# Scores of three batches as float16 products of stacked halves, with operands transposed by DMA

## The chip, the core and the metric
The kernel runs on one NeuronCore of a Trainium2 chip. The core has five engines, each with a queue of its own that it works off in order: TensorE (PE, matmuls, results in PSUM), VectorE (DVE), ScalarE (ACT), GpSimd (POOL, which cannot reach PSUM) and SyncE (SP), which here issues every DMA. The metric is the device time of one execution in microseconds (us).

## What is computed
Causal attention for 4 batches of 12 heads, then an MLP with a squared ReLU:

```
batch, n_heads, seq, head_dim = (4, 12, 448, 64)
scores = scale * np.matmul(q, k.transpose(0, 1, 3, 2))      # causal mask: -1e9 above the diagonal
attn = np.exp(scores - max);  attn = attn / (sum + 1e-09)
x = np.matmul(attn, v)  ->  (batch * seq, n_heads * head_dim) = (1792, 768)
h = x @ w_in;  r = np.maximum(h, 0.0);  g = r * r           # w_in is 768 x 2048
out = g @ w_out                                             # w_out is 2048 x 768, all float32
```

## The kernel before
**Pairs.** Attention goes by pairs of heads: 6 per batch, 24 in all, numbered i. A sequence of 448 is cut into 4 blocks of 112 rows. For a pair, `pair_load` fetches q, k and v into the tile `raw` (two sets, used in turn); `pair` transposes q and k on PE (L570, four blocks each) into PSUM and copies them out as float32 (`qT`, `kT`, L538 on ACT or L539 on DVE). In these tiles head 0 of the pair lies on partitions 0 to 63 and head 1 on 64 to 127.

**Scores and softmax.** For block c the scores of both heads, (c+1)*112 columns wide, are two float32 matmuls over 64 partitions each (L594), one in either half of the array's rows. The trace shows each as two entries. DVE adds the mask and takes the row's extreme in one custom instruction (L599), ACT takes the exponential and its sum (L603). The result is scaled and split into a float16 high half (`hi`) and a low half (`lo`) in the tile `psrc`; a DMA transposition (L556) turns both halves of a head into `pT`. The values (L651) are three float16 products: high by high, high by low, low by high. Batch 0 does without DMA transpositions and halves: it transposes float32 on PE (L629) and multiplies in float32 (L641).

**MLP.** Tokens go in sub-blocks of 256 or 128 columns, eight in all. The first layer (L918) is 16 units of 18 float16 matmuls; each unit is followed by ReLU (L929), square (L936 or L938) and the split into halves `g` (`hi` L397 on ACT, `lo` L405). The second layer (L954) is matmuls of 384 columns. Weights are loaded as raw words, narrowed (L721 to L736) and split, before the first sub-block can start.

**Who sets the order.** Every piece is handed to a planner (`Plan`) with its cost on each engine that may do it, what it reads and writes, and a due time. `Plan.order` lists the pieces by a model of the queues; the due times and a bias per engine come from the table `PR`. A split may go to ACT, DVE or POOL (`hi`), or DVE or POOL (`lo`); the planner picks. On POOL a low half of a scaled source is two instructions (L413 and L415). For SP the planner reckons a time `ISSUE` that an issue holds the queue, longer for the transpositions of pT. What it has ordered stands fixed in the program.

Of the kernel before, what the change touches and what calls it, by code (L numbers as in the profile page):

```python
# [29 lines left out]
    "m_L2": 2404805, "m_fac": -4350124, "m_ghi": 179886, "m_glo": -223927, "m_msq": 1943718, "m_ob": 5617141,  # L30
    "m_relu": -2665863, "m_sig": 3771052, "m_sq": -634180, "m_tau": 1847951, "wi_wl": 351942, "wi_wn": -1179075,
    "wi_wq": 1731582, "wo_wl": 2402465, "wo_wn": -983095, "wo_wq": -76879, "ws_wn": 4319096, "wt_wn": 1234225,
    "a0_P.copy@act": -2272, "a0_P.copy@dve": 3583, "a0_P.nrm@act": -308, "a0_P.nrm@dve": 3448, "a0_P.nrm@pool": -1037,
    "a0_qk.copy@act": -4902, "a0_qk.copy@dve": -890, "a0_x.top@act": 4549, "a0_x.top@dve": 5350,
    "m_ghi.hi@act": -5477, "m_ghi.hi@dve": -2320, "m_ghi.hi@pool": -5555, "m_glo.lo@dve": -384,
    "m_glo.lo@pool": -5962, "m_relu.@act": -4403, "m_relu.@dve": 5641, "m_sq.@act": -2058, "m_sq.@dve": 782,
    "m_sq.@pool": -1987, "ws_wn.hi@act": -3852, "ws_wn.hi@dve": -6000, "ws_wn.hi@pool": -3283, "ws_wn.lo@dve": -212,
    "ws_wn.lo@pool": 3600, "wt_wn.hi@act": -2079, "wt_wn.hi@dve": -3096, "wt_wn.hi@pool": -1467,
# [27 lines left out]
class Plan:  # L66
# [3 lines left out]
    ISSUE = {False: 475.0, True: 650.0}  # L70

    def __init__(self):
        self.ops = []
        self.heavy = set()
        self.last_w = {}
        self.last_r = {}
        self.rings = {}
        self.spots = {}
        self.port = []
        self.bias = []  # L80
        self.kind = []
# [63 lines left out]
    def order(self):  # L145
# [31 lines left out]
        warm, busy, edge = False, 0.0, self.WINDOW  # L177
        while done < n:
# [38 lines left out]
            if e == "sp":  # L217
                free[e] = t + self.ISSUE[i in self.heavy]
# [64 lines left out]
def attention_relu2_kernel(  # L283
# [32 lines left out]
    GB = [7]  # L316

# [18 lines left out]
    n_kT = maker("kT", 2)  # L336
    n_p32 = maker("p32", 2)
    n_pT = maker("pT", 3)
# [7 lines left out]
    n_l3 = maker("l3", 2)  # L346
# [15 lines left out]
    n_s = lambda b, j: spot(f"s{j}{b == 0}", SB[b == 0][j])  # L362
# [14 lines left out]
    junk = const.tile([128, VN // NPAIR], BF16, name="junk")  # L377
# [6 lines left out]
    def one(e, ns, fn, reads, writes, due, heavy=False, port=False):  # L384
        i = plan.add({e: ns}, fn, reads, writes, due, port=port)
        if heavy:
            plan.heavy.add(i)
# [663 lines left out]
```

## Time and profile before
| | us |
|---|---|
| median of 3 runs | 713.72 (710.7 to 714.43) |
| profiled execution | 715.77 |
| its span, first to last instruction | 714.0 |
| mean granted TensorE clock, share of full speed | 0.943 |

The span is cut below into stages. Busy time is the union of what an engine's instructions took. PEld is PE's weight load, which runs beside its matmuls. The granted clock (PEclk) is a share of 2.4 GHz; it is 1.2 GHz where it is 0.5.

### The profile page before, as it was taken

The page shows a single profiled execution, that of the slowest core. Times are in us where ns is not written, and L with a number is a line of the kernel's source. Part 1 is how long each engine was busy: PE and PEld are TensorE (multiplying, and loading weights), DVE is VectorE, ACT ScalarE, POOL GpSimd, SP SyncE. Part 2 cuts the span into 40 slices and gives each one's busy share as a digit, 9 for nine tenths or more (in the row PEclk, how much of TensorE's full clock was granted, in tenths as well). Part 3 has the DMA queues.
Part 4 walks back from the last instruction along what each step waited for, and adds up shares of the span by engine and source line. Part 5 has one row for each costly group of instructions (what it writes and reads, how often), then busy time and mean ns, then how long its engine had stood idle before and what let it go on. Part 6 is the DMA issues. An engine that isn't in the chain of part 4 may idle for free.

```text
span 714.0 us, 13829 instructions
## 1 busy us (share of the span) xinstructions
PE 658.6 (92%) x5182; PEld 465.0 (65%) x5182; DVE 325.8 (46%) x933; ACT 423.7 (59%) x1211; POOL 266.9 (37%) x382
## 2 busy tenths in 40 slices
PE   5877776799999899999999999999989899999998
PEld 3554544587666666787757756767656778776864
DVE  4999799889884555316320235123633110200000
ACT  2788978789876774774546664348645524414410
POOL 4232333215410326468348654447545202202200
PEclk9876767689999999999999999999999899999999
DMA  9997767545476664443365345435451300000000
GB/s 249 290 279 283 262 236 264 133 91 110 86 134 135 135 125 99 96 85 81 80 127 115 66 97 108 85 59 98 96 96 47 61 2 12 12 12 23 12 12 33
DMA packets 184866, 79.04 MB, mean 111 GB/s; under 512 B 173792, under 2 KB 179680, under 8 KB 184800
## 3 DMA queue, kind: packets, MB, share of 16 engines
q1 hardware_dynamic: 184800, 78.17, 45.7%
q8 instruction: 40, 0.66, 0.4%
q14 instruction: 26, 0.21, 0.1%
HBM read 45.81 MB, written 5.51 MB: 72 GB/s over the span
## 4 chain that ended last, share of the span: by engine, by line
PE 66%; DVE 14%; DMA 9%; POOL 5%; issue 3%; ACT 2%; SPq 1%; POOLq 0%; ACTq 0%; DVEq 0%
PE bank L918 27%; PE bank L954 23%; DMA pT<-psrc 7%; PE bank L594 5%; PE bank L651 4%; DVE bank L599 3%; PE bank L570 2%; DVE wo L724 2%; POOL p L413 2%; POOL psrc L415 2%; PE bank L641 2%; DVE wi L724 1%; DMA xt<-in_moe_w_out_dram 1%; DVE psrc L410 1%; DVE wo L721 1%
## 5 line engine op out<-in xcount | busy, mean ns | idle before, releaser
L918 PE MATMUL bank<-xt,wi 128*128 128x256 f16 (+1 forms) x2304 | 235.5, 262 | 0.0
L954 PE MATMUL bank<-wo,g 128*128 128x384 f16 x1344 | 228.8, 326 | 0.0
L918 PEld LDWEIGHTS <-wi 128*128 128x128 f16 x2304 | 201.5, 99 | 36.6 <-issue 14.3
L954 PEld LDWEIGHTS <-g 128*128 128x128 f16 x1344 | 128.2, 98 | 89.9 <-issue 10.0
L405 POOL TENSOR_TENSOR g<-g,g 128x256 f16<-128x256 f32 (+1 forms) x128 | 82.0, 650 | 197.2 <-ACT g L397 101.7
L599 DVE CUSTOM_DVE_ANT_0 bank<-bank,mask 112x112 f32<-112x112 f32 (+1 forms) x192 | 82.3, 472 | 128.8 <-PE bank L594 126.7
L603 ACT ACTIVATE p<-bank,nm 112x112 f32<-112x112 f32 (+1 forms) x192 | 93.3, 491 | 65.8 <-DVE nm L599 38.4
L594 PE MATMUL bank<-kT,qT 64*112 64x112 f32 (+3 forms) x384 | 78.0, 464 | 7.4 <-ACT p L603 4.4
L929 ACT ACTIVATE r<-bank 128x256 f32<-128x256 f32 (+1 forms) x128 | 45.0, 354 | 58.9 <-PE bank L918 58.0
L964 ACT ACTIVATE ob<-bank,fac 128x384 f32<-128x384 f32 x28 | 16.2, 579 | 82.5 <-PE bank L954 82.4
L397 ACT ACTIVATE psrc<-p,nm 112x448 f16<-112x448 f32 (+3 forms) x140 | 63.6, 524 | 0.4 <-ACT p L603 0.2
L415 POOL TENSOR_TENSOR psrc<-p,psrc 112x112 f16<-112x112 f32 (+3 forms) x76 | 53.8, 707 | 6.3
L936 ACT ACTIVATE g<-r 128x256 f32<-128x256 f32 (+1 forms) x122 | 46.8, 388 | 11.7 <-POOL g L405 7.0
L413 POOL TENSOR_SCALAR p<-p,nm 112x112 f32<-112x112 f32 (+3 forms) x76 | 43.5, 572 | 26.8 <-ACT psrc L397 26.8
L397 ACT ACTIVATE g<-g 128x256 f16<-128x256 f32 (+1 forms) x123 | 46.0, 386 | 10.7 <-PE bank L954 8.9
L594 PEld LDWEIGHTS bank<-kT,qT 64*112 64x112 f32 x384 | 31.4, 180 | 27.8 <-ACT p L603 10.9
L651 PE MATMUL bank<-pT,vp 112*64 112x336 f16 (+3 forms) x432 | 34.7, 295 | 12.2 <-DMA pT<-psrc 12.2
L410 DVE SCALAR_TENSOR_TENSOR psrc<-p,nm,psrc 112x336 f16<-112x336 f32 (+3 forms) x68 | 37.7, 592 | 10.5 <-ACT psrc L397 7.0
L651 PEld LDWEIGHTS <-vp 112*64 112x64 f16 x432 | 24.6, 114 | 24.3 <-issue 19.6
L603 ACT ACTIVATION_READ_ACCUMULATOR p<-bank,nm 112x1 f32 x192 | 38.1, 198 | 0.0
L736 POOL TENSOR_TENSOR wo<-wo,l 128x512 int32<-128x512 int32 (+1 forms) x16 | 20.0, 1253 | 44.3 <-DVE wo L724 9.2
L629 PE MATMUL bank<-ident,p 112*112 112x112 f32 x120 | 28.2, 394 | 6.2 <-ACT p L530 4.3
(120 smaller groups left out, 641.3 us busy)
## 6 DMA issues: line engine op xcount, KB each, us to landing
raw<-in_moe_w_out_dram SPq DMA_DIRECT2D x8, 768.0 KB, 5.1
xt<-in_moe_w_out_dram SPq DMA_DIRECT2D x8, 768.0 KB, 5.4
xt<-in_moe_w_in_dram SPq DMA_DIRECT2D x11, 512.0 KB, 6.2
out_dram<-ob SPq DMA_DIRECT2D x28, 192.0 KB, 2.0
raw<-in_moe_w_in_dram SPq DMA_DIRECT2D x9, 512.0 KB, 6.6
vn<-in_v_dram SPq DMA_DIRECT2D x18, 224.0 KB, 3.9
raw<-in_q_dram SPq DMA_DIRECT2D x36, 112.0 KB, 2.4
raw<-in_k_dram SPq DMA_DIRECT2D x36, 112.0 KB, 2.7
```

The lines of the kernel that those rows point to most:

```text
L397: nc.scalar.activation(out=o, in_=i, func=ACTF.Copy, scale=s)
L405: return plan.add({"dve": dve_ns(n), "pool": pool2_ns(n)}, lambda e: engines[e].tensor_tensor(out=out(), in0=in_(), in1=top(), op=ALU.subt ...
L413: nc.gpsimd.tensor_scalar(out=in_(), in0=in_(), scalar1=scale(), scalar2=1.0, op0=ALU.mult, op1=ALU.mult)
L415: nc.gpsimd.tensor_tensor(out=out(), in0=in_(), in1=top(), op=ALU.subtract)
L594: nc.tensor.matmul(out=ss[j].ap[0:P, 0:w], lhsT=q32.ap[r, c * P:w], rhs=k32.ap[r, 0:w], start=True, stop=True)
L599: one("dve", dve_ns(w, 1, 1) - 10, lambda e, c=c, w=w, s=s, j=j: nc.vector.tensor_tensor_reduce(out=s.ap[0:P, 0:w], in0=s.ap[0:P, 0:w], in ...
L603: one("act", act_ns(w, True, 1, True), lambda e, c=c, w=w, b0=b0, s=s, j=j: nc.scalar.activation(out=p32[j].ap[:, b0:b0 + c + 1, :].rearra ...
L651: nc.tensor.matmul(out=pv.ap[j * D:(j + 1) * D, kc * P:S], lhsT=vp.ap[:, hv, vb:vb + D], rhs=pT[j].ap[0:P, hp * NSL + x:hp * NSL + x + w, ...
L918: nc.tensor.matmul(out=h.ap[:, 0:n], lhsT=wi_hl(ci, hw)[:, ms], rhs=x[:, kd, hx, off:off + n], start=(kd == 0 and hw == 0 and hx == 0), st ...
L929: nc.scalar.activation(out=r.ap[:, 0:n], in_=h.ap[:, 0:n], func=ACTF.Relu)
L936: nc.scalar.activation(out=g32.ap[:, 0:n], in_=r.ap[:, 0:n], func=ACTF.Square)
L954: nc.tensor.matmul(out=o.ap[:, 0:HALF], lhsT=g[:, kf, hg, tt * 128:(tt + 1) * 128], rhs=wo_hl(kf, hw)[:, hh * HALF:(hh + 1) * HALF], start ...
```

## The change
For batches 1 to 3 (`F16S`) the scores become float16 products. Batch 0 stays as it was.

- `pair_norm`: the sums of squares of q and k of a pair (two Squares on ACT), added over partitions by a float32 matmul of two columns, give two powers of two; the score scale becomes a value in a tile (`sc`) instead of a number in the instruction.
- q and k, scaled by these, are split into halves (`qs`: 64 columns high, 64 low per head and block). A DMA transposition each makes `qT` and `kT`, whose 128 partitions are the high half stacked on the low half of one head. Two more DMAs write a copy of `kT` with the halves swapped.
- Each score block of each head is then two float16 matmuls over all 128 partitions, one with `kT` and one with the swapped copy. Each has one PSUM bank of two that are used in turn, instead of one bank per head.
- q and k are loaded by one DMA each, not two. `pT` has 2 buffers instead of 3. The third place of the narrowing (`l3`) now lies in the tile `qs`.
- The planner reckons 3500 ns for the issue of a pT transposition (650 before), 1300 for one of q or k, 650 for a swap, and 93 ns (`TURN`) whenever PE goes to or from a split array.
- The table `PR` has new numbers throughout, so that the whole order and the choice of engines are new.

```diff
...
-    "bias_dve": 329, "bias_act": -2161, "bias_pool": -229, "T0": -215719, "RAMP": 92933, "B1": 32241, "S1": 125326,
+    "bias_dve": -299, "bias_act": -4977, "bias_pool": 5919, "T0": -127481, "RAMP": 67524, "B1": 235234, "S1": 65078,
...
-    ISSUE = {False: 475.0, True: 650.0}
+    ISSUE = 475.0
+    TURN = 93.0
...
+    S16 = [1, 2]
...
+    F16S = [False, True, True, True]
...
+    n_qs = maker("qs", 2)
...
-    n_pT = maker("pT", 3)
+    n_pT = maker("pT", 2)
...
+    def pair_norm(i):
+        raws = raw_of(i)
+        due = ("a", 2 * i, "nrm")
+        ss, sc = n_ss([128, 8], I32), n_sc([128, 8], I32)
+        for n in range(2):
+            one("act", act_ns(512, acc=True), lambda e, n=n: nc.scalar.activation(
+                out=junk[0:P], in_=raws[n][0], func=ACTF.Square,
+                accum_out=ss.ap[0:P, n:n + 1].bitcast(F32)), raws[n][1], [(ss, n)], due)
+        ps = n_t(1)
+        one("pe", 310, lambda e: nc.tensor.matmul(
+            out=ps.ap[0:P, 0:2], lhsT=ones_f[0:P, 0:P], rhs=ss.ap[0:P, 0:2].bitcast(F32), start=True, stop=True),
+            [(ss, 0), (ss, 1)], [ps], due)
...
+        pow2(lambda: ps.ap[0:P, 0:2], P, 2, up, dn, [ps], [(sc, "up"), (sc, "dn")], due)
...
-        one("sp", 2500, lambda e: nc.sync.dma_start_transpose(out=pT.ap, in_=ps.rearrange("p a d -> p (a d)")),
-            [pk + (c, z) for c in range(NCH) for z in range(2)] + ["pads"], [pT], due, True)
+        one("sp", 500, lambda e: nc.sync.dma_start_transpose(out=pT.ap, in_=ps.rearrange("p a d -> p (a d)")),
+            [pk + (c, z) for c in range(NCH) for z in range(2)] + ["pads"], [pT], due, 3500.0)
...
+            qs, ks = [n_qs([128, 2 * NCH, 128], F16) for _ in range(2)]
+            qT, kT = n_qT([128, 2 * NCH, P], F16), n_kT([128, 4 * NCH, P], F16)
...
+            for t, s_, key in ((qT, qs, qT), (kT, ks, (kT, 0))):
+                one("sp", 300, lambda e, t=t, s_=s_: nc.sync.dma_start_transpose(
+                    out=t.ap[:, 0:2 * NCH, :], in_=s_.ap[0:P].rearrange("p a d -> p (a d)")), [(s_, 0), (s_, 1)], [key], due, 1300.0)
+            for z in range(2):
+                one("sp", 320, lambda e, z=z: nc.sync.dma_start(
+                    out=kT.ap[z * D:(z + 1) * D, 2 * NCH:4 * NCH, :], in_=kT.ap[(1 - z) * D:(2 - z) * D, 0:2 * NCH, :]),
+                    [(kT, 0)], [(kT, 1 + z)], due, 650.0)
...
+                    def scores16(e, c=c, s=s, j=j):
+                        for z in range(2):
+                            a = z * 2 * NCH + j * NCH
+                            nc.tensor.matmul(
+                                out=s.ap[0:P, 0:(c + 1) * P], lhsT=qT.ap[:, j * NCH + c, :],
+                                rhs=kT.ap[:, a:a + c + 1, :].rearrange("p a t -> p (a t)"), start=(z == 0), stop=(z == 1))
```

How the order moves is shown at three places, each in the middle of the MLP of a middle batch. Line numbers of the changed kernel are its own: L996 is L918, L1032 is L954, L728 is L651, L592 is L556, L415, L421 and L426 are the `hi` and `lo` instructions, L663 the float16 scores.

PE before, where a pair's second transposition and its first score block stand between two units of the first layer (`bank` numbers are PSUM banks, `xt_147` is x):

```order
L918 MATMUL bank_135<-xt_147,wi 128x256
L570 MATMUL bank_127<-ident,raw 128x112 x4
L594 MATMUL bank_119<-kT,qT 112x112
L594 MATMUL bank_123<-kT,qT 112x112
L918 LDWEIGHTS wi
```

and in the changed kernel, two score blocks of one head between a piece of the second layer and the values of an earlier pair:

```order
L1032 MATMUL bank_149<-wo,g 128x384
L663 LDWEIGHTS qT
L663 MATMUL bank_125<-kT,qT 112x112
L663 LDWEIGHTS qT
L663 MATMUL bank_125<-kT,qT 112x112
L663 LDWEIGHTS qT
L663 MATMUL bank_129<-kT,qT 112x224
L663 LDWEIGHTS qT
L663 MATMUL bank_129<-kT,qT 112x224
L728 LDWEIGHTS vp
L728 MATMUL bank_121<-pT,vp 64x448
```

The transposing group is gone from PE, and each block has two products, one after the other, into one bank.

SP before, one pair's worth of its queue (`psrc_150` and `psrc_151` are the sources of the two heads):

```order
L556 DMA_TRANSPOSE pT<-psrc_150 128x26x112
L556 DMA_TRANSPOSE pT<-psrc_151 128x26x112
L968 DMA out_dram<-ob 128x384
L524 DMA raw<-in_v_dram 112x8x64
L520 DMA raw<-in_k_dram 112x4x64 x2
L520 DMA raw<-in_q_dram 112x4x64 x2
```

and in the changed kernel:

```order
L592 DMA_TRANSPOSE pT<-psrc_156 128x26x112
L611 DMA_TRANSPOSE qT<-qs 128x8x112
L611 DMA_TRANSPOSE kT<-qs 128x8x112
L540 DMA raw<-in_v_dram 112x8x64
L592 DMA_TRANSPOSE pT<-psrc_156 128x26x112
L614 DMA kT<-kT 64x896 x2
L540 DMA raw<-in_q_dram 112x8x64
L540 DMA raw<-in_k_dram 112x8x64
```

Two transpositions and two swapping copies per pair have come into the same queue, and the copies wait there for the transposition of kT.

POOL before, in the same part of the program (`p_3378` holds exponentials, `g` the MLP's halves):

```order
L405 TENSOR_TENSOR g<-g_3632,g 128x256
L413 TENSOR_SCALAR p_3378<-p_3378,nm 112x112
L415 TENSOR_TENSOR psrc_151<-p_3378,psrc_151 112x112
L413 TENSOR_SCALAR p_3378<-p_3378,nm 112x224
L415 TENSOR_TENSOR psrc_151<-p_3378,psrc_151 112x2x112
L405 TENSOR_TENSOR g<-g_3664,g 128x256
```

and DVE in the changed kernel:

```order
L415 TENSOR_SCALAR psrc_156<-p_3560,nm 112x112
L558 SCALAR_TENSOR_TENSOR sc<-sc 112x1
L421 TENSOR_TENSOR g<-g_3670,g 128x256
L421 TENSOR_TENSOR g<-g_3676,g 128x256
L426 SCALAR_TENSOR_TENSOR psrc_157<-p_3441,nm,psrc_157 112x2x112
L646 ISA bank_129,nm<-bank_129,mask,sc 112x224
L646 ISA nm 112x1
L426 SCALAR_TENSOR_TENSOR psrc_157<-p_3441,nm,psrc_157 112x4x112
L426 SCALAR_TENSOR_TENSOR psrc_156<-p_3560,nm,psrc_156 112x112
```

The low halves of g and of the softmax, which POOL did before, stand in DVE's queue between its masks. POOL's whole list shrinks from 387 rows to 40.

## Rows read from the trace of the kernel before
**Rows 1.** The page's first part: busy us (share of the span) xinstructions of each engine.
```profile
PE 658.6 (92%) x5182; PEld 465.0 (65%) x5182; DVE 325.8 (46%) x933; ACT 423.7 (59%) x1211; POOL 266.9 (37%) x382
```
**Rows 2.** Windows: from:to, length, busy per engine (instructions), granted clock, DMA share, GB/s.
```profile
0.00:145.00 145.00, 105.51 (x630) 70.19 (x631) 126.25 (x337) 107.14 (x296) 47.09 (x41) 0.76 0.82 247
145.00:200.00 55.00, 53.69 (x442) 39.77 (x440) 48.68 (x119) 51.64 (x131) 19.74 (x20) 0.98 0.48 97
145.00:560.00 415.00, 403.64 (x3425) 284.37 (x3423) 189.48 (x570) 270.85 (x797) 197.86 (x307) 0.99 0.49 99
560.00:714.00 154.00, 149.47 (x1129) 110.39 (x1128) 10.07 (x27) 45.72 (x119) 21.97 (x34) 0.98 0.04 14
```
**Rows 3.** Waits of PE: us in total, times, longest.
```profile
PE bank L651 <- DMA pT<-psrc: 12.2, 9, 2.7
```
**Rows 4.** Timeline of PE in a middle pair: start, us, what.
```profile
341.29 2.14 PE L918 MATMUL bank<-xt,wi 128*128 128x256 f16 x18
343.36 0.82 PE L594 MATMUL bank<-kT,qT 64*112 64x336 f32 x4
...
347.74 1.01 PE L594 MATMUL bank<-kT,qT 64*112 64x448 f32 x4
348.68 2.14 PE L918 MATMUL bank<-xt,wi 128*128 128x256 f16 x18
350.65 0.55 PE L570 MATMUL bank<-ident,raw 112*128 112x112 f32 x4
351.04 2.13 PE L918 MATMUL bank<-xt,wi 128*128 128x256 f16 x18
353.01 0.28 PE L486 MATMUL bank<-s,ones_f 128*128 128x1 f32 x2
353.22 0.45 PE L594 MATMUL bank<-kT,qT 64*112 64x112 f32 x4
353.60 2.14 PE L918 MATMUL bank<-xt,wi 128*128 128x256 f16 x18
```
**Rows 5.** Timeline of PE in a sub-block of 128 columns.
```profile
215.69 2.17 PE L918 MATMUL bank<-xt,wi 128*128 128x128 f16 x36
```
**Rows 6.** Groups by form, ACT: count, then busy us, mean ns of one, idle before.
```profile
L464 ACT ACTIVATION_READ_ACCUMULATOR junk<-vn 128x1 f32 x18 | 3.5, 196 | 0.0
L397 ACT ACTIVATE vp<-raw,vst 112x512 f16<-112x512 f32 x5 | 3.6, 716 | 0.0
L538 ACT ACTIVATE qT<-bank 128x448 f32<-128x448 f32 x18 | 9.8, 542 | 20.4 <-PE bank L570 13.9 <-PE bank L594 6.5
```
**Rows 7.** Timeline of DVE: low halves of the softmax and what follows each.
```profile
160.02 0.56 DVE L410 SCALAR_TENSOR_TENSOR psrc<-p,nm,psrc 112x336 f16<-112x336 f32 x1
160.50 1.00 DVE L410 SCALAR_TENSOR_TENSOR wo<-wo,wst 128x768 f16<-128x768 f32 x1
...
181.93 0.68 DVE L410 SCALAR_TENSOR_TENSOR psrc<-p,nm,psrc 112x448 f16<-112x448 f32 x1
182.52 0.75 DVE L410 SCALAR_TENSOR_TENSOR wi<-wi,wst 128x512 f16<-128x512 f32 x1
```
**Rows 8.** Groups by form, DVE.
```profile
L410 DVE SCALAR_TENSOR_TENSOR psrc<-p,nm,psrc 112x448 f16<-112x448 f32 x21 | 16.1, 768 | 1.6 <-ACT psrc L397 1.6
...
L672 DVE SCALAR_TENSOR_TENSOR xt<-bank,xt 128x448 f16<-128x448 f32 x18 | 11.2, 623 | 18.0 <-ACT xt L668 17.7
...
L672 DVE SCALAR_TENSOR_TENSOR xt<-bank,vst,xt 128x448 f16<-128x448 f32 x6 | 4.1, 680 | 0.0
```
**Rows 9.** Source line L556: duration ns min/median/max of the issue, and landing.
```profile
L556 SPq DMA_TRANSPOSE pT<-psrc x36: 3400/3534/4518, 158.2 to 553.9; - x36
...
DMA to landing us min/median/max: 5.3/5.5/7.3
```
**Rows 10.** Timeline of SP's queue: start, us that the issue holds it, what.
```profile
234.25 0.31 SPq L524 DMA_DIRECT2D raw<-in_v_dram  x1
...
235.78 0.97 SPq L520 DMA_DIRECT2D raw<-in_q_dram  x2
```

More of the change, by code (lines that the diff above doesn't have):

```diff
@@ L79, in __init__ @@
         self.port = []
+        self.tiled = set()
+        self.wait = {}
         self.bias = []
@@ L176, in order @@
         done = 0
-        warm, busy, edge = False, 0.0, self.WINDOW
+        warm, busy, edge, split = False, 0.0, self.WINDOW, False
         while done < n:
@@ L226, in order @@
                         busy, edge = 0.0, edge + self.WINDOW
+                    if (i in self.tiled) != split:
+                        split = not split
+                        dur += self.TURN
                     if not warm:
@@ L382, in attention_relu2_kernel, with one @@
     xf = xt[1].rearrange("p k h t -> p (k h t)")
-    def one(e, ns, fn, reads, writes, due, heavy=False, port=False):
+    def one(e, ns, fn, reads, writes, due, wait=None, port=False, tiled=False):
         i = plan.add({e: ns}, fn, reads, writes, due, port=port)
-        if heavy:
-            plan.heavy.add(i)
+        if wait:
+            plan.wait[i] = wait
+        if tiled:
+            plan.tiled.add(i)
         return i
@@ L517, in pair_load @@
             t, keys = raw_of(i)[n]
-            if n < 2:
+            if n < 2 and not F16S[b]:
                 for h in range(2):
@@ L563, in pair @@
         due = ("a", 2 * i, "qk")
[L564 to L574 removed]
+        q3 = lambda t: t.rearrange("p (a d) -> p a d", d=D)
@@ new lines, in pair, with soft @@
+        scl = (lambda: sc.ap[0:P, 4:5].bitcast(F32)) if F16S[b] else (lambda: -1.0 / float(D) ** 0.5)
+        sk = [(sc, "s")] if F16S[b] else []
+        def soft(c, j, s):
+            w, b0, due = (c + 1) * P, c * (c + 1) // 2, ("a", 2 * i + j + 0.05 * c, "sc")
+            one("dve", dve_ns(w, 1, 2 if F16S[b] else 1) - 10, lambda e: nc.vector.tensor_tensor_reduce(
+                out=s.ap[0:P, 0:w], in0=s.ap[0:P, 0:w], in1=mask[:, S - w:S], scale=scl(),
+                scalar=3.0e38, op0=ALU.add, op1=ALU.min, accum_out=f32(nm[j], c, c + 1)),
+                [s, "mask"] + sk, [s, (nm[j], c)], due)
+            one("act", act_ns(w, True, 1, True), lambda e: nc.scalar.activation(
+                out=p32[j].ap[:, b0:b0 + c + 1, :].rearrange("p a t -> p (a t)"), in_=s.ap[0:P, 0:w], func=ACTF.Exp,
+                scale=-1.0, bias=f32(nm[j], c, c + 1), accum_out=f32(sm[j], c, c + 1)),
+                [s, (nm[j], c)], [(p32[j], c), (sm[j], c)], due)
@@ new lines, in pair, with scores @@
+        if F16S[b]:
+            for j in range(2):
+                for c in range(NCH):
+                    s = n_s(b, 0)
+                    def scores16(e, c=c, s=s, j=j):
[4 more added lines that the diff above has]
+                                rhs=kT.ap[:, a:a + c + 1, :].rearrange("p a t -> p (a t)"), start=(z == 0), stop=(z == 1))
+                    one("pe", 2 * mm_ns((c + 1) * P), scores16, [qT, (kT, 0), (kT, 1), (kT, 2)], [s],
+                        ("a", 2 * i + j + 0.05 * c, "sc"))
+                    soft(c, j, s)
+        else:
+            for c in range(NCH):
+                ss = [n_s(b, j) for j in range(2)]
+                def scores(e, c=c, ss=ss):
+                    for j in range(2):
+                        r = slice(j * D, (j + 1) * D)
+                        nc.tensor.matmul(
+                            out=ss[j].ap[0:P, 0:(c + 1) * P], lhsT=f32t(q32)[r, c * P:(c + 1) * P],
+                            rhs=f32t(k32)[r, 0:(c + 1) * P], start=True, stop=True)
+                one("pe", mm32_ns((c + 1) * P) + 95, scores, [q32, k32], ss, ("a", 2 * i + 0.05 * c, "sc"), tiled=True)
+                for j in range(2):
+                    soft(c, j, ss[j])
@@ L656, in pair @@
         due = ("a", 2 * i + 1, "val")
-        if b:
-            one("pe", 1600, values16, [(vp, 0), (vp, 1)] + pT, [pv], due)
+        if F16V[b]:
+            one("pe", 1550, values16, [(vp, 0), (vp, 1)] + pT, [pv], due, tiled=True)
         else:
-            one("pe", 2050, values, raws[2][1] + [(p_, a) for p_ in pT for a in range(0, NB10, 4)], [pv], due)
+            one("pe", 2050, values, raws[2][1] + [(p_, a) for p_ in pT for a in range(0, NB10, 4)], [pv], due, tiled=True)
         due = ("a", 2 * i + 1, "x")
@@ L671, in pair @@
                  [pv] + xr, xk, due, "top")
-        one("dve", dve_ns(S, 1, 0 if b else 1), lambda e: nc.vector.scalar_tensor_tensor(
+        one("dve", dve_ns(S, 1, 0 if F16V[b] else 1), lambda e: nc.vector.scalar_tensor_tensor(
             out=xs[:, 1, o:o + S], in0=pv.ap[:, 0:S], scalar=xup(), in1=xs[:, 0, o:o + S], op0=ALU.mult, op1=ALU.subtract),
@@ L978, in attention @@
             for n in (i, i + 1) if b else ():
-                if n in pairs and n not in loaded:
+                if n in pairs and n not in norms:
                     pair_load(n)
-                    loaded.add(n)
-            pair(i)
-    loaded = set()
+                    norms[n] = pair_norm(n) if F16S[b] else None
+            pair(i, norms.get(i))
+    norms = {}
     def consts(e):
```

110 lines of the change are left out of this document (54 added, 56 removed), and 32 rows, old and new, of the table PR.

## Prediction
> **What bounds the kernel now.** I read the page's totals first: TensorE (PE) is busy 92% of 714.0 us, the others 37 to 65% [rows 1]. That average hides three stages, so next the windows [rows 2]. Up to 145 us PE is busy 105.5 us at a granted clock of 0.76, while VectorE (DVE) is busy 126 of 145 us: batch 0 and the narrowing of the weights, paced by DVE. From 145 to 560 us PE is busy 403.6 of 415 us at a clock of 0.99: the MLP of the first batches runs, mixed with the attention of batches 1 to 3. From 560 us on only MLP is left, PE again at 97%. So 569 of 714 us go at the pace of PE's stream. PE's waits say the same: the largest is 12.2 us, for pT, nine times [rows 3].
>
> In such a stream a group costs not its printed duration but the distance from its start to the next start, and the timeline of one pair shows it [rows 4]. A float32 score group (four entries: two heads, two each) over 112 columns runs from 353.22 to 353.60, 0.38 us; over 448 from 347.74 to 348.68, 0.94; in between I go by columns, 0.57 for 224 and 0.75 for 336. A transposing group (q or k) takes 350.65 to 351.04, 0.39. Eighteen 256-column matmuls of the MLP take 1.97 us (351.04 to 353.01), but 2.07 where a score group follows (341.29 to 343.36): going over to the half-height form costs 0.10.
>
> **What the change removes from PE,** per pair of batches 1 to 3 (18 pairs): scores 0.38 + 0.57 + 0.75 + 0.94 = 2.64, two transposing groups 0.78, two entries of 0.10 (the other score groups here follow something else than an MLP group). Together 3.62 us.
>
> **What it adds to PE.** Sixteen float16 products, 2 heads x 2 x (112 + 224 + 336 + 448) = 4480 columns. At the rate of the 256-column stream (1.97 us for 4608 columns, 0.43 ns a column) that is 1.92. Each product loads its weights; the nearest row is 36 MLP matmuls of 128 columns, each with a load of its own, in 2.17 us, 0.060 apiece [rows 5], so a load hides even behind 128 columns and I charge none. If each of the 16 loads showed for as long, 0.96 more. The norm's float32 sum over two columns is like the pair of L486 from 353.01 to 353.22, 0.21. Sum 2.13, saved 1.49 a pair, **27 us over 18 pairs**; with every load showing, 10 us. A gain beyond that is bounded by what is removed: 18 x 3.62 = 65 us.
>
> The Trainium skill speaks against this edit: its page "TensorEngine Tiling (Array Packing)", sections "Theoretical Speedup" and "When to Use Tiling", says that a product over at most 64 rows should run as two tiles side by side, for up to twice the speed, and the change gives those tiles up. By that rule alone (an estimate from the page: what is saved by float16 is lost again by the tiles) the scores stay at 2.64 a pair, the saving falls to 14 us and the time would be about 706. The row of the 448-column group decides otherwise: both heads take 0.94 us there, and as four float16 products of 448 columns they take 0.77 at 0.43 ns, so the tiled float32 form is the dearer one.
>
> **What moves to the other engines.** The planner picks the engine of each split; in the new order GpSimd (POOL) keeps the weight additions, the edges of xt and six instructions more. What follows is counted in the two orders.
> ScalarE (ACT), 270.9 us of the middle stage now [rows 2]. Added: 36 Squares over 512 columns, like a 512-column split 0.72, and 0.2 for each sum's read-out [rows 6], 33; 36 high halves of q and k, 26; 13 more of v, 9; six copies to xt, 3. Gone: 24 copies out of PSUM, 0.54 each, 13; 16 softmax halves that go to DVE, by columns 0.5, 8. Net +50.
> DVE, 189.5 us now. Here I price by starts: a low half of 336 columns ran from 160.02 to 160.50, 0.48, one of 448 from 181.93 to 182.52, 0.59 [rows 7], so 0.11 per 112 columns and 0.42 in the mean. Added: 75 low halves of softmax, 32; 49 of q, k and v at 0.65, 32; five small ones a pair for the norm, between nothing and the 0.26 of a 112-column half, at 0.16, 14; 20 high halves, 8; the score scale as a pointer instead of a number, 0.06 by the two forms of L672 (680 and 623 ns) [rows 8], on 144, 8; low halves of g, which POOL did: no row shows these on DVE; the bounds are 0.26 (112 columns) and 0.59 (448), by columns 0.40 for 256. Gone: 24 copies and splits at 0.54, 13.
> MLP moves too. In the old order 612 first-layer and 474 second-layer matmuls stand behind the last values group, in the new one 1044 and 726. By 0.109 (180 of 256 columns), 0.060 (252 of 128) and 0.164 (252 of 384, by columns) that is 76 us of PE. So the last stage grows from 154 to 230 us, and the middle one shrinks to 415 - 27 - 76 = **312 us of PE**. Within these ACT has 270.9 + 50 less 24 MLP units (the last window has 34 in 45.7 us; 14 of the 24 are half as wide), 27: 294 us, 94%. DVE has, with 70 low halves of g (26), 189.5 + 107 = 296 us, 95%; by whole durations (the 448-column half takes 0.77 on its own [rows 8], 1.3 times its 0.59 here) what is added is 139 and the sum 329.
> This is the weak point. For cover there is one stretch: from 145 to 200 us ACT was busy 94% and DVE 89%, and PE still 98% [rows 2]. I charge the middle stage 2% for new waits, **6 us**; the bounds are 0 and the rival below.
>
> **The queue of SyncE.** A transposition of pT holds the queue 3.53 us and lands after 5.5 [rows 9]; a plain load takes 0.31 (v) or about 0.5 (half of q) [rows 10]. New are 36 transpositions of 8 blocks of columns (pT has 26) and 36 copies that swap the halves of kT; q and k become one load each. Bounds for a short transposition are 0.31 and 3.53; by blocks it is 1.1, which I take. A swap costs a load, and once a pair it waits in the queue until kT has landed, 5.5 - 3.53 = 2 us. Sum: 36 x 3.53 + 36 x 1.1 + (36 + 54) x 0.31 + 18 x 2 = 231 us of 312, 74%, against 36 x 3.53 + 72 x 0.5 + 18 x 0.31 = 169 of 415 now; with the upper price 318. Behind a waiting swap stand loads and the next pT, and PE's values wait for pT. The planner now reckons 3.5 us for that issue, where it had 0.65, which speaks for fewer than 12.2 us of waits; the fuller queue speaks for more. I leave them.
> The first 145 us lose batch 1's first scores but keep DVE's narrowing; I leave them, within 5 us.
>
> **The sum.** 145 + 312 + 230 + 6 = 693 us of span, or 714 - 27 + 6. The profiled execution took 715.8, 1.8 over its span and 2 over the median of 713.7, so span and median nearly coincide. **Forecast 693 us**, its own range 681 to 706.
>
> **Rivals.**
> *The full gain.* Nothing new is lost and the waits for pT go: 714 - 27 - 12 = 675. For it: the order reckons with dearer transpositions. Against: three fuller queues. 0.11.
> *Given back.* The 27 us turn into PE's waits for softmax halves or pT: 707 to 717. For it: DVE at 95%. Against: PE's 98% from 145 to 200 us. 0.13.
> *DVE sets the pace of the middle stage* (the other side). If the added work costs whole durations, 329 us, and the queue fills to 93%, between its best stretch (89%) and its reckoned share (95%), the stage takes 354 us: 145 + 354 + 230 = 729. It decides once the stage passes 339 us, 9% over PE's 312. 0.12. The Trainium skill's page "SBUF — State Buffer", section "SBUF: two separate sides", would soften it: DVE and GpSimd lock each other out of one shared pair of ports, so with POOL idle DVE should run freer. No row here shows that alone.
> *SyncE sets the pace:* at 3.53 us for a short transposition 318 us and some waits more, past 339 too: 720. 0.06.
> That leaves 0.58 for the forecast.
>
> **Chances.** About 0.5% is what a measurement of this kernel can tell from no change: faster is below 710.1, slower above 717.3. Faster 0.58 + 0.11 + 0.05 of the second rival: 0.74. Same 0.08 of it and 0.01 of the last two: 0.09. Slower 0.17. The range, 670 to 720, leaves out some 0.14 above and 0.04 below.
>
> **What the next profile would show.** Score products of 1.9 us a pair by starts; no transposing groups after 145 us; PE over 95% busy until the last values group, near 463 us. Wrong if PE waits there for softmax halves while DVE's or ACT's queue is never empty; if 112-column products stand 0.1 us apart (loads show); if a short transposition holds SyncE over 2 us; or if the MLP starts later than 150 us.

## The result, and the profile after

The changed kernel takes 688.22 us (median of 4 runs, 687.76 to 691.4) against 713.09 for the kernel before; the ratio is 0.966, 95% interval 0.963 to 0.970. The forecast was 693, range 670 to 720. The profiled execution has a span of 686.0 us, 28.0 under that of before. One run of e7 below (697.54 us at a granted clock of 0.909) fell into a slower state and is left out of e7's figures.

The page's totals and the windows of its stages (length, busy time per engine with instructions, granted clock, DMA share, GB/s) answer to [rows 1, 2]:

```profile
PE 627.5 (91%) x5074; PEld 461.8 (67%) x5074; DVE 417.4 (61%) x1272; ACT 453.3 (66%) x1308; POOL 55.4 (8%) x56
```

```profile
0.00:142.00 142.00, 100.30 (x605) 66.49 (x606) 122.77 (x332) 109.26 (x294) 45.47 (x38) 0.78 0.82 245
142.00:462.00 320.00, 306.87 (x2673) 231.84 (x2674) 260.42 (x842) 268.78 (x800) 9.96 (x18) 0.99 0.88 167
220.00:380.00 160.00, 152.50 (x1354) 114.63 (x1352) 133.43 (x463) 135.38 (x425) 5.35 (x11) 1.00 1.02 189
462.00:686.00 224.00, 220.31 (x1798) 163.46 (x1796) 34.16 (x100) 75.23 (x215) 0.00 (x0) 1.00 0.04 15
```

The stages lie where the forecast put them: first MLP product near 142 us, last values group at 462, then 224 us of MLP. New are two things. In the middle TensorE is busy 306.9 of 320 us, 96%, a little less than before. And the DMA share (the time of the packets that start in a window, over 16 engines' time, so that it can pass 1), 0.49 in the middle before, is 1.02 from 220 to 380 us.

The score products themselves cost what was reckoned. The timeline of TensorE (start, us, what) shows one head's four blocks, two products each:

```profile
441.55 0.26 PE L663 MATMUL bank<-kT,qT 128*112 128x112 f16 x2
...
442.62 0.35 PE L663 MATMUL bank<-kT,qT 128*112 128x224 f16 x2
...
443.79 0.45 PE L663 MATMUL bank<-kT,qT 128*112 128x336 f16 x2
...
445.05 0.54 PE L663 MATMUL bank<-kT,qT 128*112 128x448 f16 x2
```

Each step of 2 x 112 columns adds 0.09 to 0.10 us, that is 0.42 ns a column, 1.9 us for the 4480 columns of a pair. Such a row lasts longer than that, since it runs to the end of its last product and not to the next start.

To see where the 28 us came from, I took the starts of all matmuls in the trace from the first MLP product on, gave each matmul the distance to the next start, and added these up by the function that issues it, so that a wait counts to the matmul ahead of it (us):

| | before | after | float32 scores (e1) | one product (e5) | SyncE work (e11) |
|---|---|---|---|---|---|
| first MLP product starts at | 144.6 | 141.9 | 143.4 | 142.3 | 143.5 |
| both MLP layers | 449.4 | 452.7 | 448.7 | 460.9 | 457.0 |
| scores, transposing q and k, pair norms | 62.3 | 46.3 | 64.0 | 34.8 | 49.5 |
| values of batches 1 to 3 | 45.7 | 32.5 | 33.7 | 38.7 | 47.1 |

So the gain is 16.0 us at the scores, 13.2 at the values and 2.7 ahead of the MLP, less 3.3 in the MLP's layers. The first was forecast, as 27 less 6 for new waits; the second was not.

### The profile page after: what moved, and what is told of

It reads as the page before. It is cut to its first block, busy times and chain, and to the rows that moved or that the text cites. A ratio compares the mean times of both kernels' runs of the same rounds, so it can differ in the third digit from the quotient of the medians.

```text
span 686.0 us, 13763 instructions
## 1 busy us (share of the span) xinstructions
PE 627.5 (91%) x5074; PEld 461.8 (67%) x5074; DVE 417.4 (61%) x1272; ACT 453.3 (66%) x1308; POOL 55.4 (8%) x56
## 4 chain that ended last, share of the span: by engine, by line
PE 56%; ACT 17%; DMA 13%; DVE 9%; issue 2%; SPq 2%; POOL 0%; ACTq 0%; POOLq 0%; DVEq 0%
PE bank L1032 22%; PE bank L996 22%; ACT p L650 4%; DMA pT<-psrc 4%; DMA kT<-qs 4%; DMA raw<-in_k_dram 3%; PE bank L663 2%; DVE bank L646 2%; ACT p L566 2%; PE bank L728 2%; ACT psrc L413 2%; PE bank L718 2%; ACT junk L548 2%; PE bank L706 1%; ACT qs L413 1%
## 5 line engine op out<-in xcount | busy, mean ns | idle before, releaser
L996 PE MATMUL bank<-xt,wi 128*128 128x256 f16 (+1 forms) x2304 | 234.1, 261 | 0.4 <-ACT r L1007 0.4
L1032 PE MATMUL bank<-wo,g 128*128 128x384 f16 x1344 | 230.2, 326 | 1.1 <-DVE g L421 1.1
L996 PEld LDWEIGHTS <-wi 128*128 128x128 f16 x2304 | 203.2, 99 | 25.2 <-issue 1.2
L1032 PEld LDWEIGHTS <-g 128*128 128x128 f16 x1344 | 130.0, 98 | 82.2 <-DVE g L421 1.5
L421 DVE TENSOR_TENSOR g<-g,g 128x256 f16<-128x256 f32 (+1 forms) x128 | 46.6, 386 | 153.7 <-ACT g L413 88.8
L646 DVE CUSTOM_DVE_ANT_0 bank<-bank,mask,sc 112x112 f32<-112x112 f32 (+3 forms) x144 | 70.4, 512 | 13.4 <-PE bank L663 10.9
L426 DVE SCALAR_TENSOR_TENSOR psrc<-p,nm,psrc 112x224 f16<-112x224 f32 (+3 forms) x143 | 69.2, 507 | 10.6 <-ACT psrc L413 10.1
L1042 ACT ACTIVATE ob<-bank,fac 128x384 f32<-128x384 f32 x28 | 16.2, 582 | 86.2 <-PE bank L1032 86.1
L413 ACT ACTIVATE psrc<-p,nm 112x336 f16<-112x336 f32 (+3 forms) x124 | 56.9, 516 | 12.2 <-DMA pT<-psrc 11.1
L663 PE MATMUL bank<-kT,qT 128*112 128x112 f16 (+3 forms) x288 | 52.5, 284 | 7.1 <-ACT p L650 6.6
L1014 ACT ACTIVATE g<-r 128x256 f32<-128x256 f32 (+1 forms) x128 | 47.1, 387 | 4.8 <-DVE g L421 3.4
L663 PEld LDWEIGHTS <-qT 128*112 128x112 f16 x288 | 32.8, 130 | 16.9 <-issue 10.6
L650 ACT ACTIVATION_READ_ACCUMULATOR p<-bank,nm 112x1 f32 x192 | 38.3, 200 | 0.0
L728 PE MATMUL bank<-pT,vp 112*64 112x448 f16 (+3 forms) x432 | 30.9, 284 | 2.3 <-DMA pT<-psrc 2.2
L426 DVE SCALAR_TENSOR_TENSOR qs<-raw,sc,qs 112x512 f16<-112x512 f32 x36 | 27.7, 777 | 8.1 <-ACT qs L413 7.1
L706 PEld LDWEIGHTS bank<-ident,p 112*112 112x112 f32 x120 | 19.3, 199 | 18.6 <-ACT p L566 11.6
L413 ACT ACTIVATE qs<-raw,sc 112x512 f16<-112x512 f32 x36 | 25.5, 716 | 8.6 <-DMA kT<-qs 5.4
L728 PEld LDWEIGHTS <-vp 112*64 112x64 f16 x432 | 22.0, 109 | 12.4 <-issue 7.3
```

Source lines behind the costliest of these rows:

```text
L413: nc.scalar.activation(out=o, in_=i, func=ACTF.Copy, scale=s)
L421: return plan.add({"dve": dve_ns(n), "pool": pool2_ns(n)}, lambda e: engines[e].tensor_tensor(out=out(), in0=in_(), in1=top(), op=ALU.subt ...
L426: nc.vector.scalar_tensor_tensor(out=out(), in0=in_(), scalar=scale(), in1=top(), op0=ALU.mult, op1=ALU.subtract)
L646: one("dve", dve_ns(w, 1, 2 if F16S[b] else 1) - 10, lambda e: nc.vector.tensor_tensor_reduce(out=s.ap[0:P, 0:w], in0=s.ap[0:P, 0:w], in1= ...
L650: one("act", act_ns(w, True, 1, True), lambda e: nc.scalar.activation(out=p32[j].ap[:, b0:b0 + c + 1, :].rearrange("p a t -> p (a t)"), in ...
L663: nc.tensor.matmul(out=s.ap[0:P, 0:(c + 1) * P], lhsT=qT.ap[:, j * NCH + c, :], rhs=kT.ap[:, a:a + c + 1, :].rearrange("p a t -> p (a t)") ...
```

## Experiments

The theory at first was that of the prediction: from the first MLP product on the time follows TensorE's stream. Its rivals: the new order and table alone bring the gain; VectorE, ScalarE or SyncE set the pace.

**e1: the old form in the new order.**
```diff
-    F16S = [False, True, True, True]
+    F16S = [False, False, False, False]
```


> The changed kernel with its table and its planner, but the scores of batches 1 to 3 again as float32 products of q and k turned by TensorE. Theory (the form of the scores on TensorE's stream is what pays, 13 us of it after new waits, and 10 us more come from pT being there in time): the form's part goes, so 700 to 715 us, with the waits of the values products for pT still under 5 us. Rival (the new order, table and planner alone bring the gain): 684 to 692 us. Rival (the move of work from GpSimd to VectorE and ScalarE brings it): under 695 us as well, since q and k halves leave those engines altogether.


Measured: 704.45 us, 0.987 of before (0.982 to 0.991). Under this table the form is worth 16.2 us and the rest of the change 8.6. The table above has both: the scores cost 64.0 again, while the values keep their 33.7. So the values' 12 us (45.7 to 33.7) belong to the new order, planner and choice of engines, and order alone is not the gain.

**e2: the old table. e3: the price of MLP steps changed a little. e4: the old price of pT.**
```diff
-    "bias_dve": -299, "bias_act": -4977, "bias_pool": 5919, "T0": -127481, ...
+    "bias_dve": 329, "bias_act": -2161, "bias_pool": -229, "T0": -215719, ...
```
```diff
-    "RATE": 0.0038
+    "RATE": 0.0040
```
```diff
-        one("sp", 500, lambda e: nc.sync.dma_start_transpose(out=pT.ap, ...
-            ... + ["pads"], [pT], due, 3500.0)
+        one("sp", 2500, lambda e: nc.sync.dma_start_transpose(out=pT.ap, ...
+            ... + ["pads"], [pT], due, 650.0)
```


> The changed kernel with the table of numbers of the kernel before (entries that it lacks count as zero). Theory (the form pays, the table only keeps stalls small): 690 to 706 us, still under the 713 of before. Rival (the table is the gain): 710 us or more. In either case the score products themselves should keep their 1.9 us a pair on TensorE, and what is lost should stand as waits in front of them and of the values products.

> A control: one number of the table, the price by which MLP steps fall due, goes from 0.0038 to 0.0040. No cost on the chip changes, the order does in places. Theory (the gain is the form's, any sane order has most of it): 684 to 698 us. Rival (the gain hangs on this one order): over 700 us. The distance from 688 is what any re-planned experiment must exceed before it says something.

> The changed kernel, with the planner's price of the big transposition pT set back to what it was before (650 ns of SyncE and 2500 ns of transfer, for 3500 and 500). Theory (pT is there in time because the planner now counts its 3.5 us of SyncE): the waits of the values products for pT come back from 2.2 us to 8 or more, and the time goes to 693 to 700 us. Rival (pT is earlier because the low halves are now made on VectorE instead of GpSimd): waits for pT stay under 4 us and the time within 684 to 692.


Measured: e2 710.91 us, ratio 0.997 (0.994 to 1.000); e3 687.11, 0.963 (0.959 to 0.968); e4 717.07, 1.007 (1.004 to 1.010). The nudge costs nothing, so a small change of order need not show. The other two lose 23 and 29 us. e2 comes out where its rival had it (710 us or more): with the old table the float16 form gains nothing on the kernel before that stands clear of noise (2 us), so the form's 16.2 us hold for the new table alone. The new table came with the float16 scores, and the old one has no entries for what is new, so neither figure is the form's worth by itself. e4 lies beyond both of its forecasts. TensorE's waits (us, times, longest), first of e2, then of e4:

```profile
PE bank L661 <- ACT p L648: 14.3, 25, 2.1
PE bank L726 <- DMA pT<-psrc: 8.0, 4, 6.1
```

```profile
PE bank L663 <- ACT p L650: 16.4, 19, 2.5
PE bank L728 <- DMA pT<-psrc: 7.5, 9, 1.4
```

These waits, in front of the scores and of the values, were 6.6 and 2.2 us in the changed kernel. They are 13.5 us more in e2 and 15.1 in e4, over half of what was lost; the rest is not accounted for. In e4 the planner takes 3.5 us of SyncE for 0.65, and so may have laid out the queues for halves and tiles that are not there yet; that is argued. What e4 does not show is whether the old price would have done the same with a table made for it.

**e5: one product of each score block. e6: a third bank. e7: more work on VectorE. e8: g's low halves on GpSimd.** All keep the order.
```diff
-                        for z in range(2):
+                        for z in range(1):
...
-                                rhs=kT.ap[:, a:a + c + 1, :].rearrange("p a t -> p (a t)"), start=(z == 0), stop=(z == 1))
+                                rhs=kT.ap[:, a:a + c + 1, :].rearrange("p a t -> p (a t)"), start=True, stop=True)
```
```diff
...
-        return plan.spot([i], bank[i])
...
+        at = [1, 2, 3][n % 3] if places is S16 else i
+        return plan.spot([i], bank[at])
...
```
```diff
...
+                if F16S[b]:
+                    nc.vector.tensor_copy(out=spare[0:P], in_=ones_f[0:P])
...
```
```diff
+            if self.kind[i] == "lo" and self.ops[i][4][0] == "m":
+                e = "pool"
```


> The changed kernel, order kept, with only the first of the two products of each score block (the cross products of high and low halves are left out of the scores). It takes 2240 columns a pair off TensorE: at 0.43 ns a column 0.96 us a pair, 17 us in all. Theory (from the first MLP product to the last, the time follows TensorE's stream of products): 670 to 677 us. Rival (the blocks of scores are paced by VectorE and ScalarE, which hand back their two banks): 681 to 688 us, with the waits for ScalarE's exponential grown from 6.6 us to 15 or more.

> The changed kernel, order kept, with the score blocks of batches 1 to 3 going round three PSUM banks instead of two (the third is the one of the small norm products, which move to its last columns). Theory (some 13 us of the form's gain stand as waits and long steps in front of score products, because a bank comes back late from ScalarE): the 6.6 us of waits for ScalarE's exponential fall under 3 and the time to 676 to 684 us. Rival (those long steps have another cause, the bank is not short): 686 to 690 us.

> The changed kernel, order kept, with a copy of 128 float32 columns to a spare tile on VectorE behind each of the 144 minimum reductions of batches 1 to 3; by the row of 128 column subtractions (285 ns) and the shortest of similar work, estimated 0.2 to 0.3 us each, 29 to 43 us of VectorE in all. It changes no result. Theory (TensorE's stream sets the time, VectorE has slack in the middle): 688 to 700 us. Rival (VectorE sets the pace of the middle): 712 to 730 us.

> The changed kernel, order kept, with the low halves of g (128 subtractions, 46.6 us on VectorE) on GpSimd again, where they took 721 ns each for 256 columns in the kernel before. Theory (VectorE is not what sets the time, and the second layer's products come long after their halves): 685 to 693 us. Rival (the move from GpSimd to VectorE is part of the gain, since g's halves come 0.3 us sooner): 695 us or more. Rival (VectorE sets the pace): under 680 us.


Measured: e5 689.85 us (686.55 to 691.09), e6 687.22 (686.55 to 687.79), e7 690.12 (687.19 to 690.76), e8 694.43 (694.17 to 698.11).

e5 breaks the theory. Of the 17 us taken off TensorE nothing arrives: in the table the scores fall by 11.5 us, but the values take 6.2 more and the MLP 8.2. Its granted clock is not the reason: the run with a clock of 0.953, within the changed kernel's 0.950 to 0.957, took 686.55 us. The windows from 420 to 460 us, of the changed kernel and of e5, show TensorE with less to do, waiting:

```profile
420.00:460.00 40.00, 39.90 (x325) 28.30 (x324) 22.26 (x65) 24.36 (x69) 0.00 (x0) 1.00 0.83 156
```

```profile
420.00:460.00 40.00, 36.32 (x288) 25.47 (x286) 22.45 (x65) 24.46 (x69) 0.00 (x0) 0.96 0.77 145
```

The sign of the rival, that VectorE and ScalarE pace the blocks, came in part: score products wait longer for ScalarE's exponential, 13.0 us against 6.6 (15 or more was expected).

```profile
PE bank L663 <- ACT p L650: 13.0, 22, 1.6
```

Neither is it the banks: in e6 the waits of score products for ScalarE's exponential fall from 6.6 to 2.1 us (3.8 come up at the norm products, which share the third bank), and the time is the same. Nor VectorE: e7's 144 copies have 33.5 us of duration, and the time grows by 1.9, inside its own scatter. In e8 the move of g's low halves to VectorE proves worth 6.2 us, in this order; e1, which keeps that move, may have part of its 8.6 from it.

**What the trace says instead.** I set the values groups of successive pairs against the two pT transpositions of each pair. First SyncE's queue of the changed kernel (start, us; a row with x2 holds both heads of the pair), then the values on TensorE:

```profile
427.41 7.81 SPq L592 DMA_TRANSPOSE pT<-psrc  x2
438.86 7.35 SPq L592 DMA_TRANSPOSE pT<-psrc  x2
450.48 7.23 SPq L592 DMA_TRANSPOSE pT<-psrc  x2
```

```profile
425.76 1.62 PE L728 MATMUL bank<-pT,vp 112*64 112x448 f16 x24
...
437.21 1.62 PE L728 MATMUL bank<-pT,vp 112*64 112x448 f16 x24
...
448.44 2.05 PE L728 MATMUL bank<-pT,vp 112*64 112x448 f16 x24
...
460.28 1.62 PE L728 MATMUL bank<-pT,vp 112*64 112x448 f16 x24
```

The values end at 427.38, and the next pair's first transposition starts at 427.41; they end at 438.83, and it starts at 438.86; 450.49 and 450.48. There are two pT tiles, one a head, so the next pair's can be written only when the values have read them. The second transposition leaves the queue at 435.22, 446.21 and 457.71, and the values start 2.0 to 2.6 us later, about when it lands. That closes a ring, a chain in which each step waits for the one before and the last lets the first go on: two issues 7.2 to 7.8, landing 2.0 to 2.6, values 1.6 to 2.1, 11.5 us a pair. Of TensorE's work only the values stand in it. In 10 of 17 pairs of the changed kernel the first transposition starts within 0.5 us of the end of the values ahead, most of them after 281 us. A whole turn without other delays, 11.0 to 12.4 us from one pair's values to the next, stands in 6 of the 17. In the others it is 13.4 to 30.8: other transfers stand between the two issues (283 to 297 us), or MLP work ahead of the values (384 to 415 us). In the kernel before, with three tiles, the first transposition starts 6.8 to 14.9 us after the values ahead, in all 17.

Earlier, the queue itself is full. SyncE from 239 to 267 us:

```profile
238.77 0.59 SPq L540 DMA_DIRECT2D raw<-in_q_dram  x1
239.88 1.11 SPq L614 DMA_DIRECT2D kT<-kT  x2
241.10 8.25 SPq L592 DMA_TRANSPOSE pT<-psrc  x2
249.45 1.25 SPq L611 DMA_TRANSPOSE qT<-qs  x1
250.75 1.29 SPq L611 DMA_TRANSPOSE kT<-qs  x1
252.14 0.53 SPq L540 DMA_DIRECT2D raw<-in_v_dram  x1
252.73 0.57 SPq L540 DMA_DIRECT2D raw<-in_k_dram  x1
253.97 1.34 SPq L614 DMA_DIRECT2D kT<-kT  x2
255.41 8.14 SPq L592 DMA_TRANSPOSE pT<-psrc  x2
263.65 0.53 SPq L540 DMA_DIRECT2D raw<-in_v_dram  x1
```

There is hardly a gap, and 14.3 us from one pair's pT to the next. In e5 (the changed kernel with one product of each score block) the pairs' values end at 225.6, 240.4, 256.6, 270.6 and 284.5 us, in the changed kernel at 225.1, 239.6, 253.5, 266.9 and 280.8: with half the score products the pairs come no faster.

The transposition also holds its source. `psrc` has two tiles too, one a head, and the softmax halves of the next pair can be written only when pT has been read out of it. ScalarE's halves, first of the changed kernel, then of e5 and of e11 (below), with the idle time ahead of them at the end:

```profile
L413 ACT ACTIVATE psrc<-p,nm 112x336 f16<-112x336 f32 (+3 forms) x124 | 56.9, 516 | 12.2 <-DMA pT<-psrc 11.1
L413 ACT ACTIVATE psrc<-p,nm 112x336 f16<-112x336 f32 (+3 forms) x124 | 57.0, 517 | 19.4 <-DMA pT<-psrc 19.3
L414 ACT ACTIVATE psrc<-p,nm 112x336 f16<-112x336 f32 (+3 forms) x124 | 56.9, 513 | 26.1 <-DMA pT<-psrc 24.2
```

So the pT transposition holds up ScalarE as well, and behind it, as far as can be argued, the score products that wait for its exponentials.

In e1, the old form with two pT tiles, the queue has gaps and from 220 to 430 us the ring is open. Its SyncE, pT alone, and its values:

```profile
244.44 7.28 SPq L592 DMA_TRANSPOSE pT<-psrc  x2
...
263.34 7.20 SPq L592 DMA_TRANSPOSE pT<-psrc  x2
...
279.32 4.52 SPq L592 DMA_TRANSPOSE pT<-psrc  x1
```

```profile
239.06 1.62 PE L728 MATMUL bank<-pT,vp 112*64 112x448 f16 x24
...
254.06 1.89 PE L728 MATMUL bank<-pT,vp 112*64 112x448 f16 x24
...
273.47 1.62 PE L728 MATMUL bank<-pT,vp 112*64 112x448 f16 x24
```

The transpositions start 3.8, 7.4 and 4.2 us after the values end, and TensorE is busy 40.00 of 40 us in each window of 40 us from 220 to 460, as in this one:

```profile
260.00:300.00 40.00, 40.00 (x324) 26.43 (x322) 27.24 (x97) 29.28 (x90) 0.00 (x0) 1.00 0.65 131
```

There its stream still sets the time. At 433.5 and 445.3 us two transpositions of e1 do start right behind the values, with TensorE full all the same: there the closed ring cost nothing, since TensorE had as much to do in a turn. From 420 to 460 us the changed kernel stands at that point too (11.5 us a turn, TensorE busy 39.90 of 40 us).

**e9, e10: loads and swaps issued by GpSimd. e11: more issues on SyncE. e12: swaps alone on GpSimd.** All keep the order. The expectations were written when SyncE's full queue had been seen, the ring not.
```diff
-            one("sp", dma_ns(P * 2048, 256), lambda e, t=t, a=a: nc.sync.dma_start(
+            one("sp", dma_ns(P * 2048, 256), lambda e, t=t, a=a: (nc.gpsimd if b else nc.sync).dma_start(
...
-                one("sp", 320, lambda e, z=z: nc.sync.dma_start(
+                one("sp", 320, lambda e, z=z: nc.gpsimd.dma_start(
```
e10 adds e5's edit to this, and e12 is its second part alone. e11:
```diff
...
+            for x in range(2 * n - 2 * H, 2 * n - 2 * H + 2):
+                nc.sync.dma_start(out=spare[0:1, x:x + 1], in_=ones_f[0:1, 0:1])
+            nc.sync.dma_start_transpose(out=pT.ap, in_=ps.rearrange("p a d -> p (a d)"))
```


> After the run with one product the theory that the middle follows TensorE's stream is in doubt: with 17 us of products gone the pairs still ended 14 us apart between 225 and 281 us. New theory: SyncE's queue sets that pace; its transfers' issues fill 34 to 36 of every 40 us from 220 to 380 us (14 to 21 in the kernel before). Here the order is kept, but the loads of q, k and v of batches 1 to 3 (54, some 0.54 us each on SyncE) and the swaps (36, 0.58 us) are issued by GpSimd, which is nearly idle: some 2.8 us a pair come off SyncE. New theory: pairs end 12 to 13 us apart there and the time is 674 to 683 us. Rival (ScalarE and VectorE, 34 to 36 of 40 us busy there, set the pace): 686 to 690 us, 14 us a pair. Rival (the 16 DMA engines, whose share stands at 1.0 there, set it): the same 686 to 690, with the share still at 1.0.

> The kernel with loads and swaps issued by GpSimd, and with only the first of the two products of each score block (the cross products of the halves are left out of the scores). If SyncE's queue is what kept the run with one product from gaining, TensorE's 17 us now show: 664 to 676 us, and at least 8 us under the same kernel with both products. Rival (ScalarE and VectorE set the pace): 685 to 692 us, no difference between one product and two.

> The changed kernel, order kept, with two more transfers of 4 bytes into a spare tile on SyncE's queue ahead of each of the 36 transpositions pT: by the shortest issues on this queue (0.33 us) 24 us of SyncE, and next to nothing for the DMA engines or for any other engine. It changes no result. New theory (SyncE's queue sets the pace of the middle): the two thirds of the pairs that lie between 220 and 420 us pay, so 700 to 712 us. Rival (ScalarE and VectorE, or the DMA engines' bandwidth): 687 to 692 us.

> Only the 36 swaps of batches 1 to 3 are issued by GpSimd, the loads stay on SyncE, the order is kept. In the run that moved loads and swaps, GpSimd's issues stood some 3 to 4 us apart and the loads came late, so it did not answer the question about SyncE. Two swaps a pair take 2 x 0.58 us off SyncE, 21 us in all, and its waits for kT to land ahead of them (11.8 us). Theory (SyncE's queue holds up the middle; 42 us more on it cost 22 us): about half of the 21 us comes back, 674 to 682 us. Rival (the order and the other engines hold the middle as much): 685 to 690 us. Rival (the second swap lands some 3.5 us late on GpSimd's queue): over 690 us, with waits for kT in front of score products.


Measured: e9 766.81 us, e10 769.4, e11 710.45 (709.19 to 713.47), e12 692.13 (691.96 to 694.32).

e9 and e10 miss their question, and every time that was expected; one product or two makes no difference there. GpSimd's queue in e9 (start, us, what, idle time ahead):

```profile
356.36 0.86 POOL L540 DMA_DIRECT2D raw<-in_q_dram  x1 [6.34 <-DVE qs L426]
360.21 0.83 POOL L540 DMA_DIRECT2D raw<-in_k_dram  x1 [2.98 <-DVE g L421]
361.03 0.55 POOL L614 DMA_DIRECT2D kT<-kT  x1
364.30 0.53 POOL L614 DMA_DIRECT2D kT<-kT  x1 [2.72 <-issue]
```

The k load stands 3.9 us behind the q load and the second swap 3.3 behind the first, so the loads come late; TensorE then waits 41.7 us for ScalarE's sums of squares in the norms.

e11 does answer. Its SyncE, one turn of the ring:

```profile
447.03 1.22 SPq L595 DMA_DIRECT2D spare<-ones_f  x2
449.20 4.30 SPq L596 DMA_TRANSPOSE pT<-psrc  x1
453.54 1.17 SPq L595 DMA_DIRECT2D spare<-ones_f  x2
454.82 3.53 SPq L596 DMA_TRANSPOSE pT<-psrc  x1
...
461.73 3.54 SPq L596 DMA_TRANSPOSE pT<-psrc  x1
```

The 72 issues hold SyncE 0.58 us each (median), 42 us, where 24 was expected. In this turn the two ahead of the first transposition run while it would have waited for the values anyway; the two between the transpositions lie inside the ring, 1.2 us. The time grew by 22.2, 14.6 of it at the values (table), and the distance from one pair's values to the next by 1.3 us in the mean (between -0.5 and 3.4). TensorE's waits for pT rose from 2.2 to 10.5 us. Next to e5, where 17 us less on TensorE gave nothing, this shows that the chain of pT on SyncE is on the path that sets the time. It does not part the ring from the full queue: 8 of the 22 us come in the four pairs from 225 to 281 us. Nor do the DMA engines set the pace by themselves: their share from 220 to 380 us fell to 0.94 while the time grew. Whether their load lengthens the issues of pT (3.4 to 4.8 us in the changed kernel) is open.

In e12 nothing came back and 3.9 us more were lost. That is the time of its last rival, but no score product waits for kT there. With the swaps out of the queue the first transposition starts within 0.6 us of the values ahead in all four pairs from 225 to 281 us (0.8 to 2.0 in the changed kernel), so the ring closes there as well. The pairs still end 13 to 16 us apart, since pT issues there took up to 5.5 us (4.5 before the move). Why they grew is open; the DMA share stood at 1.06 to 1.11.

A third pT tile in the changed kernel was not tried, so that the ring would open with it is argued from these runs, not shown. The rows bound what it could give. In the turns at 427, 439 and 450 us the halves for the next transposition were ready 3.3, 1.9 and 3.0 us before it started, so that a third tile could have brought it forward by no more; and TensorE stands idle for only 13.1 of the 320 us in the middle.

## Why the prediction came out right

**What bounded the kernel before.** TensorE's stream, as read: e1, with the same float32 scores, shows it at 40.00 of 40 us, and no run speaks against it.

**27 us from the form.** It measured 16.2 (e1), 16.0 in the table: 62.3 us stood there before where the sum takes away 65.2 (18 x 3.62), and 46.3 are left where it adds 38.3 (18 x 2.13). The price of the products was right, and their loads are hidden. The step that failed is that the middle stage shrinks by all that is saved on TensorE, less 6 us for new waits: 21 net, 5.0 more than came. From there on another chain, SyncE's queue with the transpositions of pT, holds the pairs' pace as much as TensorE does, and e5 shows that products taken away beyond that are worth nothing. pT with two buffers instead of three stood in the change, and neither it nor the wait of the next halves for `psrc` has a term in the sum. How much of the 5.0 us these two cost is not shown.

**pT waits left at 12.2 us.** Also wrong. TensorE waited 2.2 us for pT, as the source line of the transpositions shows (duration of the issue min/median/max, who waited, landing):

```profile
L592 SPq DMA_TRANSPOSE pT<-psrc x36: 3410/3711/4780, 172.7 to 454.2; - x36
...
  PE bank L728: 2.2, 4
...
DMA to landing us min/median/max: 5.3/5.7/7.1
```

In the new order the values come later: they start after the pair's second pT has landed in 13 of 18 pairs, in the kernel before in 7. The gain at the values, 13.2 us, was not counted; e1 puts 12 of it down to the new order, planner and choice of engines. Against the sum's 693 the form gave 5.0 us less, the values 13.2 more and the start of the MLP 2.7 more, the MLP's layers took 3.3 more and the rest 0.6: 7.0 in all, to a span of 686.0. That the number is near is in part luck, since errors of either sign stand in it.

**VectorE and ScalarE at 95%.** Measured 260 and 269 us of 320, 81 and 84%; the charge of 6 us for new waits is about the 6.6 in front of the scores, and e6 shows that more banks do not turn them into time. VectorE as the bound is ruled out by e7.

**SyncE at 74%.** The share was right, 238 of 320 us by adding up the issues, and the sizes were near: a short transposition measured 1.24 and 1.29 us (1.1 reckoned), pT 3.71 (3.53), a swap 0.59 (0.31):

```profile
L611 SPq DMA_TRANSPOSE qT<-qs x18: 1221/1240/1362, 137.8 to 409.6; - x18
L611 SPq DMA_TRANSPOSE kT<-qs x18: 1228/1292/2109, 139.2 to 411.0; - x18
...
L614 SPq DMA_DIRECT2D kT<-kT x36: 461/586/1492, 142.4 to 414.7; - x36
```

But a mean share over the middle hides that from 225 to 281 us the queue was full, and that later it stood waiting for the values, with nothing it could do. The rival "SyncE sets the pace" named the right queue, but by a price of 3.53 us for a short transposition, which measured 1.24 and 1.29, and its time of 720 did not come.

**Stages.** MLP start 141.9 (145), last values at 462 (463), tail 224 (230): right.

**Tiles or full height.** The float16 products of a pair's scores take 1.9 us by starts, as reckoned, where the tiled float32 form took 2.64. The rule of the Trainium skill's page "TensorEngine Tiling (Array Packing)", section "Theoretical Speedup", by which, in the prediction's estimate, the tiles should have cost the change half its saving, is not what cut it: the 16.2 us lie near the 14 by that rule, but the part that was lost lies between the score blocks, outside the products.

## What to carry to other kernels

When an edit takes away a buffer, or puts new transfers into a queue, draw the ring that it closes (the wait for the last reader, the issue, the landing, the read), add up one turn from the rows, and set it against the time in which an item has to come; a sum of busy times per engine does not show it. When an engine is at 96%, take some work off it before believing that it is the bound. And when a planner sets the order, a wrong price for one long DMA issue can cost more than the edit gains: prices, table and form moved the time together here (e1, e2, e4).

## What was not expected of the hardware

Issues of a 4 byte transfer held SyncE 0.58 us between the transpositions, as long as a swap of 112 KB. In the rows of e9 a k load on GpSimd's queue stood 3.9 us behind the q load and the second swap 3.3 behind the first, while a swap followed a load after 0.8; what GpSimd waited for in between is not shown. With pT, qT, kT and swaps running, the DMA share was 1.02 at 189 GB/s, where [rows 2] have 0.82 at 247 GB/s. And in e5 the granted clock was 0.96 in three windows of 40 us in which the changed kernel had 1.00, with TensorE busy 35 to 38 of 40 us there; from 220 to 260 us, with 34.3 busy, it stayed at 1.00. Why it fell there is open.
